# Scalar loads on another queue, the identity at the start, ten warming products and an early branch hint in a fused attention and two-layer gated kernel

## The chip, the cores and the metric

The kernel runs on one core of a Trainium2 chip. The metric is the device time of one execution in microseconds; three executions of the kernel before took 602.41, 602.73 and 602.85, the median is 602.73. One further execution was recorded by the hardware profiler: it took 602.38 us, of which the span of its instructions is 600.6 us; the remaining 1.78 us lie around the span.

## The reference

Three steps follow each other. Step one is masked softmax attention for 2 batches and 8 heads over 768 positions with 64 features per head. A query sees the first `n_sink` keys (4) and a causal window of `window` keys (128); both are scalar inputs, so the kernel has to load them before it can build a mask.

```python
scores = scale * np.matmul(q, k.transpose(0, 1, 3, 2))
keep = is_sink | in_window            # pos < n_sink, or 0 <= row - col < window
scores = np.where(keep, scores, -1e9)
a = np.exp(scores - max); a = a / (sum(a) + 1e-9)
x = np.matmul(a, v)                   # reshaped to 1536 tokens x 512
h = x @ w_in;  x = (h * tanh(softplus(h))) @ w_out      # 512 -> 2048 -> 512
h = x @ w2_in; out = (h * clip(h + 3, 0, 6) / 6) @ w2_out
```

## The kernel before

The 1536 rows are cut into twelve units of 128 query rows. Eight units (lists `first`) run in fp32 through `first_blocks()`; the other four run as a side task (`gen_units`) beside the first layer. For a unit of the first kind, `prep` transposes k and q on TensorE (PE) against an identity matrix `ident` (line 323), ScalarE (ACT) copies the transposes out of PSUM (line 326), `scores` multiplies them (line 350), VectorE (DVE) adds a mask and takes the maximum in one instruction (line 354), and ACT takes the exponential (line 358). `turn` and `values` transpose the probabilities and multiply by v (lines 369 and 393). The first unit in the list is unit 6, which starts its batch and so needs mask `m0` only.

The two layers that follow are split-precision fp16 products (lines 737 to 739 and 782 for the first layer, 806 to 808 and 846 for the second). Their weights arrive as fp64 words by DMA from SyncE's (SP's) queue and are decoded on DVE. This body is fully unrolled.

The head of the program, in the order of the code: a table load on ACT, three small constants by memset on DVE, then `emit_params` (lines 107 to 120), which issues two small broadcast loads of the scalars on SP and turns them into fp32 values `nsw` by seven small DVE instructions; then the loads of k, q and v of the first units and of the first weights, all on SP; then `warm`, a zeroed tile, and `NWARM` products of it (line 931) whose result nobody reads; then `emit_masks` (lines 122 to 153), which makes two index matrices on GpSimd (POOL), the identity and the masks on DVE. Four further products of `warm` stand behind the first unit's transposes (line 428).

The language has a scheduler. It keeps the instructions of an engine roughly in the order of the code, but lets one that is ready in its own simulated time go ahead of one that is not; the order on each engine is fixed when the program is built, and each engine then runs its instructions in that order. `tc.keep_in_program_order(x)` ties `x` behind what the code has already given to that engine. It ties nothing else.

The end of the program (lines 987 to 1012) reduces a number of checks into one integer `bad_i`. All five engines load it (`values_load`, line 1011) and branch on it (`tc.If(bad != 0)`, line 1012): where it is not zero, `general_path` recomputes everything in a slow general form; where it is zero, as with these inputs, every engine jumps past that code to a closing sequence of semaphore steps (reported at line 1216), in which SP waits for every other engine.

## Time and profile before

| what | value |
|---|---|
| median of three executions | 602.73 us |
| profiled execution | 602.38 us |
| its span | 600.6 us |
| PE busy | 579.9 us (97%) |
| DVE busy | 457.9 us (76%) |
| ACT busy | 398.3 us (66%) |
| POOL busy | 24.3 us (4%) |
| share of the chain that ended last, by engine | PE 65%, DVE 12%, issue 10%, ACT 8%, DMA 2%, POOL 2% |

Busy time counts the instructions that compute; branches, semaphore steps and the issue of DMAs are not counted, so an engine that is held in one of these shows as idle. A name like PEq, SPq or PEldq is the sequencer of that engine, which runs those uncounted instructions. The chain that ended last is followed back from the last computing instruction, so it doesn't reach into the closing sequence. A row of the timeline that ends in a bracket tells how long the engine was idle before it and what released it.

### The profile page before, as it was taken

The numbers are of one execution on the slowest core, as the hardware profiler recorded it, in microseconds if no ns is written. First come the engines' busy times: TensorE is split into PE (matmuls) and PEld (weight loads), VectorE is DVE, ScalarE is ACT, GpSimd is POOL, SyncE is SP. The second block draws the span as 40 slices with busy tenths as digits, with TensorE's granted clock in tenths as the row PEclk, the third lists the DMA queues.
The fourth block names the chain that finished last, engine by engine and source line by source line (L and its number), as shares of the span: only waits on it lengthen the run. The fifth ranks groups of instructions, "written<-read, shape, count | busy, mean of one in ns | idle before, by whom it ended". The sixth has DMA issues, their size and how long they took to land.

```text
span 600.6 us, 11389 instructions
## 1 busy us (share of the span) xinstructions
PE 579.9 (97%) x4430; PEld 395.0 (66%) x4430; DVE 457.9 (76%) x1102; ACT 398.3 (66%) x786; POOL 24.3 (4%) x36
## 2 busy tenths in 40 slices
PE   8999999999989999899989999999999999999995
PEld 5778764444445545444434468888888888888884
DVE  5689998999375454589999999866687889865753
ACT  5998887777687776679888886434354656543442
POOL 0041000700000000000000000000000000000000
PEclk9999999999999999999999999999999999999998
DMA  9876357997334433254544442000017676300001
GB/s 182 222 162 211 108 174 198 234 263 209 90 73 82 81 61 70 39 158 140 183 168 139 142 141 71 1 1 2 1 36 257 213 267 214 135 7 1 36 1 40
DMA packets 105843, 72.26 MB, mean 120 GB/s; under 512 B 73512, under 2 KB 98088, under 8 KB 105784
## 3 DMA queue, kind: packets, MB, share of 16 engines
q1 hardware_dynamic: 105784, 71.48, 42.4%
q8 instruction: 36, 0.59, 0.4%
q14 instruction: 23, 0.19, 0.1%
HBM read 60.43 MB, written 3.15 MB: 106 GB/s over the span
## 4 chain that ended last, share of the span: by engine, by line
PE 65%; DVE 12%; issue 10%; ACT 8%; DMA 2%; POOL 2%; SPq 0%; DVEq 0%; ACTq 0%
PE acc L846 18%; PE acc L782 9%; PE h L807 7%; PE h L806 7%; PE h L808 7%; PE h L737 3%; PE h L739 3%; PE h L738 3%; DVE g L754 2%; ACT d L358 1%; DVE p L212 1%; PE o L393 1%; DVE e L749 1%; DVE d L354 1%; ACT e L745 1%
## 5 line engine op out<-in xcount | busy, mean ns | idle before, releaser
L782 PE MATMUL acc<-g,w 128*128 128x512 f16 x576 | 131.2, 379 | 6.1 <-DVE g L754 5.4
L846 PE MATMUL acc<-w,g 128*128 128x256 f16 x1008 | 113.8, 273 | 0.0
L846 PEld LDWEIGHTS <-g 128*128 128x128 f16 x1008 | 98.6, 98 | 11.4
L806 PE MATMUL h<-xt,w 128*128 128x256 f16 x384 | 104.7, 273 | 0.0
L808 PE MATMUL h<-xt,w 128*128 128x256 f16 x384 | 104.7, 273 | 0.0
L807 PE MATMUL h<-xt,w 128*128 128x256 f16 x384 | 104.7, 273 | 0.0
L782 PEld LDWEIGHTS <-w 128*128 128x128 f16 x576 | 55.4, 98 | 72.2 <-issue 7.6
L737 PE MATMUL h<-xt,w 128*128 128x512 f16 x192 | 72.8, 379 | 1.9 <-DVE mins L558 1.2
L739 PE MATMUL h<-xt,w 128*128 128x512 f16 x192 | 72.8, 379 | 0.0
L738 PE MATMUL h<-xt,w 128*128 128x512 f16 x192 | 72.8, 379 | 0.0
L810 ACT ACTIVATE e<-h,bias 128x512 f32<-128x512 f32 x48 | 32.5, 678 | 54.5 <-PE h L808 54.5
L811 DVE SCALAR_TENSOR_TENSOR e<-e,h 128x512 f32<-128x512 f32 x48 | 32.8, 683 | 41.9 <-ACT e L810 41.9
L823 ACT ACTIVATE g<-e 128x256 f16<-128x256 f32 x96 | 29.5, 354 | 28.7 <-DVE e L811 28.7
L823 ACT ACTIVATE g<-sm 128x512 f16<-128x512 f32 x48 | 30.2, 629 | 27.5 <-DVE sm L818 27.4
L749 DVE SCALAR_TENSOR_TENSOR e<-e,h 128x512 f32<-128x512 f32 x48 | 30.7, 681 | 16.8 <-ACT e L747 16.7
L824 DVE SCALAR_TENSOR_TENSOR g<-sm,g 128x512 f16<-128x512 f32 x48 | 33.0, 688 | 11.0 <-ACT g L823 10.9
L807 PEld LDWEIGHTS <-w 128*128 128x128 f16 x384 | 37.6, 98 | 4.6
L806 PEld LDWEIGHTS <-w 128*128 128x128 f16 x384 | 37.6, 98 | 4.6
L808 PEld LDWEIGHTS <-w 128*128 128x128 f16 x384 | 37.6, 98 | 4.3
L212 DVE SCALAR_TENSOR_TENSOR p<-raw,y 128x1024 int32<-128x1024 int32 x32 | 39.4, 1232 | 0.4
L740 ACT ACTIVATE e<-h 128x512 f32<-128x512 f32 x48 | 28.1, 587 | 16.2 <-PE h L739 16.2
L754 DVE SCALAR_TENSOR_TENSOR g<-e,g 128x1024 f16<-128x1024 f32 x24 | 29.4, 1223 | 8.3 <-ACT g L753 8.3
(172 smaller groups left out, 935.6 us busy)
## 6 DMA issues: line engine op xcount, KB each, us to landing
raw<-in_moe_w_in_dram SPq DMA_DIRECT2D x48, 512.0 KB, 4.2
raw<-in_moe_w_out_dram SPq DMA_DIRECT2D x48, 512.0 KB, 4.9
out_dram<-ob SPq DMA_DIRECT2D x12, 256.0 KB, 2.6
first<-in_k_dram SPq DMA_DIRECT2D x8, 256.0 KB, 4.6
first<-in_q_dram SPq DMA_DIRECT2D x8, 256.0 KB, 4.5
first<-in_v_dram SPq DMA_DIRECT2D x8, 256.0 KB, 3.0
nk<-in_k_dram SPq DMA_DIRECT2D x5, 256.0 KB, 5.0
nv<-in_v_dram SPq DMA_DIRECT2D x5, 256.0 KB
```

Source lines behind the costliest of these rows:

```text
L212: nc.vector.scalar_tensor_tensor(out=p, in0=t[:, :, 1], scalar=3, in1=y, op0=ALU.logical_shift_left, op1=ALU.bitwise_xor)
L737: nc.tensor.matmul(o, wh, x[:, 0, c, :], start=c == 0, stop=False)
L738: nc.tensor.matmul(o, wh, x[:, 1, c, :], start=False, stop=False)
L739: nc.tensor.matmul(o, wl, x[:, 0, c, :], start=False, stop=c == KD - 1)
L749: nc.vector.scalar_tensor_tensor(out=e[:, i], in0=e[:, i], scalar=2.5, in1=hps[i], op0=ALU.subtract, op1=ALU.mult)
L754: nc.vector.scalar_tensor_tensor(out=gl, in0=e, scalar=sc, in1=gh, op0=ALU.mult, op1=ALU.subtract)
L782: nc.tensor.matmul(o, l_, r_, start=first and m == 0 and x == 0, stop=last and end and x == 2, skip_group_check=True)
L806: nc.tensor.matmul(o, wh, x[:, 0, c, :], start=c == 0, stop=False)
L807: nc.tensor.matmul(o, wh, x[:, 1, c, :], start=False, stop=False)
L808: nc.tensor.matmul(o, wl, x[:, 0, c, :], start=False, stop=c == KD - 1)
L823: nc.scalar.activation(out=g[:, 0, d_], in_=src, func=AF.Copy, scale=sc)
L846: nc.tensor.matmul(a[n // 2][:, n % 2], l_, r_, start=f == fa and m == 0 and n % 2 == 0 and x == 0, stop=ends and m == 1 and x == 2 and (n ...
```

## The change

It does four things. The two scalar loads are issued on ACT's queue instead of SP's, and `emit_params` stands ahead of ACT's table load and of the constants. The two index matrices and the identity are made by a new function `emit_ident`, which is the first thing in the code, with the matrix that the identity needs made first and the identity itself under `keep_in_program_order`; `emit_masks` gets the tile with the index matrices handed over. `NWARM` is 10 instead of 12. Last, a branch hint "likely taken" is placed on all five engines ahead of the warming tile, and tied by the label `end` to the branch at line 1012.

```diff
     def emit_params():
-            nc.sync.dma_start(out=raw[:, i, :], in_=a.bitcast(I32)...)
+            nc.scalar.dma_start(out=raw[:, i, :], in_=a.bitcast(I32)...)
...
-    def emit_masks():
+    def emit_ident():
+        tmp = part_p.tile([128, 4, 128], F32, tag="part", name="tmp")
+        col, rel = tmp[:, 0], tmp[:, 1]
+        nc.gpsimd.iota(rel, pattern=[[-1, 128]], base=0, channel_multiplier=1, ...)
+        tc.keep_in_program_order(nc.vector.tensor_scalar(out=ident, in0=rel, scalar1=0.0, scalar2=None, op0=ALU.is_equal))
+        nc.gpsimd.iota(col, pattern=[[1, 128]], base=0, channel_multiplier=0, ...)
+        return tmp
+
+    def emit_masks(tmp):
         ns, wd = nsw[:, 0:1], nsw[:, 1:2]
-        tmp = part_p.tile([128, 4, 128], F32, tag="part", name="tmp")
         col, rel, ind, dg = (tmp[:, i] for i in range(4))
-        nc.gpsimd.iota(col, ...)
-        nc.gpsimd.iota(rel, ...)
-        nc.vector.tensor_scalar(out=ident, in0=rel, scalar1=0.0, scalar2=None, op0=ALU.is_equal)
...
+    tmp_m = emit_ident()
+    emit_params()
     nc.scalar.preload_act_table_set("natural_log_exp_and_others")
     nc.vector.memset(one, 1.0)
     nc.vector.memset(fifth, 0.2)
     nc.vector.memset(bias3, 3.0)
-    emit_params()
     load_first(first[0], "kq")
...
+    tc.mark_branch_hint_location("end", hint="LikelyTaken", engines=[PE, DVE, Activation, Pool, SP])
     warm = part_p.tile([128, 512], F32, tag="part", name="warm").bitcast(F16)[:, 0:512]
...
-    emit_masks()
+    emit_masks(tmp_m)
...
-    with tc.If(bad != 0):
+    with tc.If(bad != 0, label="end"):
         general_path(tc, q, k, v, nsw, w1_in, w1_out, w2_in, w2_out, out)
...
-NWARM = 12
+NWARM = 10
```

## Rows read from the trace of the kernel before

**Rows 1.** The page, part 1: busy time, share of the span and instructions of each engine.
```profile
PE 579.9 (97%) x4430; PEld 395.0 (66%) x4430; DVE 457.9 (76%) x1102; ACT 398.3 (66%) x786; POOL 24.3 (4%) x36
```
**Rows 2.** Instructions around the end, line 1012: durations in ns (min/median/max), starts in us.
```profile
L1012 ACTq COMPARE_BRANCH  x1: 50/50/50, 596.1 to 596.1; - x1
L1012 PEldq COMPARE_BRANCH  x1: 3414/3414/3414, 596.1 to 596.1; - x1
...
L1012 PEldq EVENT_SEMAPHORE  x1: 51/51/51, 599.6 to 599.6; - x1
```
**Rows 3.** The same view of the closing sequence, line 1216.
```profile
L1216 SPq EVENT_SEMAPHORE  x10: 17/28/2127, 597.2 to 600.6; - x10
```
**Rows 4.** SP's own waits from 592 us on: total us, times, longest us.
```profile
SPq L1216 <- PEq L1012: 2.1, 1, 2.1
```
**Rows 5.** The page, part 3: packets, MB and share of the instruction queue q8.
```profile
q8 instruction: 36, 0.59, 0.4%
```
**Rows 6.** Chain that ended last, 0 to 30 us: start us, us, what.
```profile
1.27 5.30 PE wp L931 x12
6.57 0.98 PE tp L323 x8
7.55 0.86 PE wp L428 x4
...
9.20 1.65 ACT d L358 x8
```
**Rows 7.** Timeline of SP's DMA issues: start us, us of issue.
```profile
0.74 0.39 SPq L110 DMA_DIRECT2D raw<-in_n_sink_dram  x1
1.20 0.41 SPq L110 DMA_DIRECT2D raw<-in_window_dram  x1
1.66 0.43 SPq L293 DMA_DIRECT2D first<-in_k_dram  x1
2.12 0.58 SPq L293 DMA_DIRECT2D first<-in_q_dram  x1
2.75 1.23 SPq L293 DMA_DIRECT2D first<-in_k_dram  x1
```
**Rows 8.** DMA issues from 2.5 to 3 us: KB, median us to landing.
```profile
first<-in_q_dram SPq DMA_DIRECT2D x1, 256.0 KB, 4.3
first<-in_k_dram SPq DMA_DIRECT2D x1, 256.0 KB, 4.9
```
**Rows 9.** Line 323, PE's semaphore waits ahead of the first two units' transposes.
```profile
L323 PEldq EVENT_SEMAPHORE  x2: 51/51/51, 5.3 to 8.9; - x2
```
**Rows 10.** Timeline of ACT, DVE and POOL, 0 to 12 us.
```profile
0.73 1.28 ACT L912 ACT_TABLE_LOAD   x1 [0.73 <-PEq L1201]
0.94 0.27 DVE L928 MEMSET warm<- 128x256 uint32 x1
1.10 0.24 POOL L127 IOTA tmp<- 128x128 f32 x1
...
4.17 0.17 DVE L113 CAST f<-raw 128x4 f32<-128x4 int32 x1 [2.94 <-DMA raw<-in_window_dram]
...
5.91 0.22 DVE L128 TENSOR_SCALAR ident<-tmp 128x128 f32<-128x128 f32 x1
...
7.15 0.60 ACT L326 ACTIVATE kt<-tp 128x512 f32<-128x512 f32 x1 [5.13 <-PE tp L323]
7.21 0.23 DVE L135 TENSOR_SCALAR m<-tmp 128x128 f32<-128x128 f32 x1
...
7.64 0.59 ACT L326 ACTIVATE qt<-tp 128x512 f32<-128x512 f32 x1
...
8.87 0.29 DVE L354 CUSTOM_DVE_ANT_0 d<-s,m 128x128 f32<-128x128 f32 x1 [0.23 <-PE s L350]
```
**Rows 11.** Stretches: us, busy of PE, PEld, DVE, ACT, POOL; granted clock, DMA share, GB/s.
```profile
595.50:600.60 5.10, 0.00 (x0) 0.00 (x0) 0.01 (x1) 0.00 (x0) 0.00 (x0) 0.66 0.07 20
0.00:12.00 12.00, 10.18 (x54) 5.59 (x56) 6.42 (x48) 5.17 (x14) 0.70 (x7) 1.00 0.95 165
```

## Prediction

> **What bounds the kernel now.** I began with the busy shares: PE computes for 579.9 of 600.6 us, 97% [rows 1]. The reader is to see that the body can't give much without less PE work, and that the change takes only two products away from PE. So I looked at what isn't the body: the first 12 us and the last 5. For the end I read the line of the final branch, the line of the closing sequence and SP's own waits [rows 2 to 4]. The stretch from 595.5 us to the end holds no computing work at all [rows 11], yet it is 5.1 us long. PE's branch at 596.1 takes 3414 ns where ACT's takes 50 [rows 2], PE's next step is at 599.6, and SP, which gathers the engines, has one semaphore step of 2127 ns [rows 3], which is its wait of 2.1 us for PE [rows 4]. For the head I read the chain that ended last, the issues on SP and the timeline [rows 6, 7, 10]: the chain starts with twelve warming products from 1.27 to 6.57, then runs through the first unit's transposes, its scores and ACT's exponentials. The DMA engines are at 0.95 over the first 12 us [rows 11], so the head has two chains side by side, PE's warming and the loads.

> **The end.** The hint adds one instruction per engine near the start, and there nothing waits for it but the warming tile's memset, so I put it at nothing on PE and at most at a branch's 0.05 us [rows 2] on DVE. What it may remove is the long branch on PE: all five engines branch at 596.1, and the others are through in about 0.05 us. If PE were as quick, its semaphore step would come at about 596.1 + (599.6 - 596.1 - 3.41) + 0.05, that is before 596.3 instead of at 599.6. That isn't the gain. SP takes its steps one after another and reaches the one that waits for PE 2.13 us before that wait ends [rows 3]; what is late next is SP itself. The gain is therefore the wait, 2.1 us [rows 4], and not the 3.36 us by which PE's branch shortens. From below it is 0, if the early hint has no effect.

> That the 3.4 us are a fetch of code is argued from three rows: the branch alone is long on PE, PE has by far the longest program (4430 products and as many weight loads [rows 1]), and the queue q8 carried 36 packets in 0.59 MB, 16 KB each [rows 5], which as a stream over the span is what a long program would ask for. [...]

> **The head.** *Scalar loads.* On SP the two scalar loads hold the queue from 0.74 to 1.66 [rows 7]. Without them the first k load is issued at 0.74, 0.92 us earlier, and every load behind it on SP moves with it. Today the first q, issued at 2.12, lands 4.3 us later at 6.4, the second unit's k, issued at 2.75, 4.9 us later at 7.65 [rows 7, 8], and PE waits for loads at 5.3 and again at 8.9 [rows 9]. All of that can move by up to 0.92. The DMA engines are full in this stretch [rows 11], so the flow moves as a whole. On ACT the two issues come ahead of the table load, 0.92 us; that load ends then at about 0.73 + 0.92 + 1.28 = 2.9, and ACT's first use is at 7.15 after 5.13 us idle [rows 10]: hidden. If it were not, it would cost the 0.92.

> *The scalars themselves* now share the DMA engines with the k load. Today the conversion on DVE starts at 4.17 and mask `m0` is finished at 7.21 + 0.23 = 7.44; it is used first at 8.87 [rows 10]. It has 1.4 us of slack. At best the scalars land as today; at worst behind the two loads that are now issued beside them, 2 x 1.23 us later (1.23 = 7.65 - 6.42, one load after another [rows 7, 8]), and `m0` comes at 9.9, a loss of 1.0 against today. Queued behind the waiting conversion on DVE are the masks and the first unit's `L354`, and ACT waits for these. The nearest row is the `window` load itself, 2.9 us from issue to use [rows 7, 10]; with half a load's delay `m0` is at 8.0, still ahead of an L354 that has moved forward by 0.5 to 8.4, and I take no loss.

> *Warming and the identity.* Twelve products take 5.30 us, 0.43 each; the four behind the transposes 0.86, 0.22 each [rows 6]. [...] The granted clock is printed as 1.00 for the whole head [rows 11], so here I go by the pace. Two products fewer are 2 x 0.43 = 0.86 us. Against it stands the identity: if DVE really does it ahead of the memset of `warm`, the memset waits for an index matrix on POOL (0.24) and for `ident` (0.22), so the warming starts up to 0.46 later [rows 10]; and if the scheduler lets the memsets go first, 0. The transposes, which follow the warming without a gap [rows 6], so start 0.40 to 0.86 earlier, at 5.5 to 6.0. Today `ident` is ready at 5.91 + 0.22 = 6.13 [rows 10], so without the edit it would be the next to hold them; made early, it is out of the way. The k load would be there at 5.3 - 0.92 = 4.4 and q at 5.5.

> [...]

> ACT copies the transposes at 7.15 and 7.64, and the scores, the maximum (8.87) and the exponentials (9.20) hang on the second copy [rows 6, 10]. Bounds of the head: +0.92 (everything moves with SP) and -1.0 (masks late). I take 0.5 us, from the middle of 0.2 to 0.86. I expect it to stay to the end, since loads, PE, ACT and DVE all move the same way and PE is full behind them.

> **Sum.** Against the profiled execution's 602.38 (span 600.6 and 1.78 around it): 602.38 - 2.1 - 0.5 = 599.8. That execution is 0.35 below the median of three, 602.73, so the time to compare is 599.8 + 0.35 = about 600.1.

> **Rivals.** (1) *The hint has no effect*: a block fetched on it is gone, or never fetched, when the branch comes. For it speak the 36 blocks that pass through the queue [rows 5]; against it that a hint which is tied to one branch by name should be kept until that branch is fetched. PE's branch stays at 3.4 us and the head alone is left: 602.73 - 0.5 = 602.2. (2) *The other side: the hint misleads the fetch.* If PE's sequencer goes for the hinted block at its first block end instead of for the next one, PE stalls there for as long as at its branch today, 3.41 us [rows 2], and since PE is full from then on [rows 1] the stall is not hidden; the hinted block is used up long before the end, so the branch stays long as well. 602.73 + 3.4 - 0.5 = 605.6. It decides if at one of the first ends of PE's blocks a gap of over 3 us stands on PE that isn't there now; nothing in this trace shows a hint, so I can't exclude it. (3) *The masks turn late* with the scalars behind the loads: 602.73 - 2.1 + 1.0 = 601.6 with a hint that works. What speaks against it is the slack of 1.4 us [rows 10].

> **How the numbers follow.** Forecast 0.60; no effect 0.22; misled fetch 0.11; late masks or an order of the scheduler's that costs about as much 0.07. Some 0.2% (1.2 us) is what a measurement of this kernel can tell from no change: faster means below 601.5, slower above 603.9. The forecast's own range is 599.3 to 601.1: a head that gives 0.92 instead of 0.5 makes 599.7, and the three executions shown lie 0.44 apart; a head that loses half of its lower bound, 0.5, makes 601.1. All of it is faster. No effect is the same, late masks are between, misled is slower: faster 0.62, same 0.26, slower 0.12. The range for all reaches from 599.3 over the second case to 602.6, and leaves out the misled fetch and the edges.

> **What would show it.** Right: PE's branch at line 1012 falls from 3414 to under 200 ns; SP's wait for PE in the closing sequence is gone, and the stretch after `bad_i` is about 3.0 us instead of 5.1; the first k load is issued at about 0.74; the transposes of line 323 start at 5.5 to 6.0 and ACT's first exponential at about 8.7. Wrong: a branch of 3.4 us again (first rival); a gap of microseconds on PE, 10 to 30 us from the start, that is not there now (second); a mask instruction on DVE as the releaser of `L354` (third). If the branch is short and the time has fallen by over 3 us, I have mistaken SP's steps for a bound that they aren't.

## The result and the profile after

The changed kernel takes 607.86 us (median of four, 605.67 to 608.95) against 602.57 for the kernel before: 1.0088 times as long, 95% interval 1.0067 to 1.011. It is slower, and its four executions spread over 3.3 us, those of the kernel before over 0.8 (over 1.4 to 2.5 us in the 9 to 23 executions taken beside the later runs). The profiled execution is the fastest of the four, 605.67 us with a span of 603.9. What is read from it below therefore accounts for 605.67 - 602.38 = 3.3 us of a loss of 5.3; the other three have a mean granted clock of 0.995 against its 0.998, and no profile shows where they lost the rest. The forecast of 600.1 missed; so did the range. The other-side rival's number, 605.6, is near the profiled execution's by chance: its mechanism is not what happened.

**The end did what was forecast.** Line 1017 is the branch now and line 1221 the closing sequence; the columns are those of [rows 2, 3].
```profile
L1017 ACTq COMPARE_BRANCH  x1: 68/68/68, 601.4 to 601.4; - x1
...
L1017 PEldq COMPARE_BRANCH  x1: 385/385/385, 601.5 to 601.5; - x1
...
L1221 SPq EVENT_SEMAPHORE  x10: 17/28/28, 602.6 to 603.8; - x10
...
L1221 PEldq BRANCH_PREFETCH_HINT  x1: 50/50/50, 0.8 to 0.8; - x1
```
PE's branch is down from 3414 ns to 385, and SP's longest step from 2127 ns to 28: the wait for PE [rows 4] is gone. The hint that did it was issued 600 us earlier, in 50 ns. The instruction queue q8 carried 35 packets instead of 36 [rows 5]: behind the last computation there is one where there were two. The stretch behind the last computation, as in [rows 11]:
```profile
600.80:604.00 3.20, 0.00 (x0) 0.00 (x0) 0.04 (x1) 0.00 (x0) 0.00 (x0) 0.53 0.09 30
```
It is 3.1 us long (up to 603.9) where it was 5.1.

**The head went the other way.** The timeline of the changed kernel, in order of time, for [rows 6, 7, 10]:
```profile
0.83 0.46 SPq L296 DMA_DIRECT2D first<-in_k_dram  x1
...
1.25 0.45 ACTq L110 DMA_DIRECT2D raw<-in_window_dram  x1
...
1.35 4.45 PE L936 MATMUL wp<-warm 128*128 128x512 f16 x10 [1.35 <-DVE ones L1002]
...
5.36 0.17 DVE L113 CAST f<-raw 128x4 f32<-128x4 int32 x1 [4.06 <-DMA raw<-in_window_dram]
...
6.83 0.22 DVE L126 TENSOR_SCALAR ident<-tmp 128x128 f32<-128x128 f32 x1
...
7.10 1.97 PE L326 MATMUL tp<-ident,first 128*128 128x128 f32 x8 [1.30 <-DVE ident L126]
...
8.86 1.84 PE L431 MATMUL wp<-warm 128*128 128x512 f16 x4
...
10.64 0.71 PE L353 MATMUL s<-kt,qt 64*128 64x128 f32 x8
```
The first k load did leave SP 0.83 us earlier. But the scalars landed 1.2 us later (conversion at 5.36, before at 4.17), and `ident` still stands behind the scalars' conversion on DVE, at 6.83. The reader is to see the bracket at 7.10: PE had finished its ten products and stood idle for 1.30 us for `ident`. Then it ran slowly: the transposes took 1.97 us and the four products 1.84. The same view of the kernel before:
```profile
6.37 1.19 PE L323 MATMUL tp<-ident,first 128*128 128x128 f32 x8
7.39 1.03 PE L428 MATMUL wp<-warm 128*128 128x512 f16 x4
```
In the changed kernel these four products start some 0.43 us apart, the lower pace, that of the twelve in [rows 6]; the four there take 0.22 each, the upper pace. What the expectations say of PE's clock in the head is read from these two paces: the granted clock is printed as 1.00 for the first 12 us here too, and no trace shows that a clock is behind them. The first scores start at 10.64 instead of 8.34.

**More was lost where nothing was edited.** Stretches of both kernels, columns as in [rows 11]; first the kernel before:
```profile
12.00:75.00 63.00, 59.84 (x590) 47.44 (x591) 52.93 (x187) 56.62 (x170) 10.84 (x17) 1.00 0.68 179
...
120.00:160.00 40.00, 38.94 (x200) 17.60 (x199) 30.13 (x43) 29.64 (x42) 0.00 (x0) 1.00 0.81 211
```
and the changed kernel:
```profile
12.00:75.00 63.00, 58.17 (x585) 47.08 (x584) 51.82 (x189) 55.77 (x169) 9.67 (x16) 1.00 0.65 171
...
120.00:160.00 40.00, 36.75 (x188) 16.30 (x187) 34.81 (x49) 28.22 (x40) 0.00 (x0) 1.00 0.91 237
```
PE is 1.7 us less busy in the fp32 attention stage and 2.2 us less from 120 to 160 us. By the start of the first product of the first layer (72.5 us before, 76.4 now) the lag has grown from 2.3 to 3.9 us, by 175 us to 5.7; at the end of the computing it is 5.3, and the end gives 2.0 back: 3.3. The traces show why to look there: up to 150 us the order of the instructions differs on all five engines, although the code there is the same. Of the kernels below, e1 (the hint alone) and e3 (all edits but the queue) have the order of before behind the head, and e2 (the queue alone) has that of the changed kernel. So it is the move of the two loads to ACT's queue that makes the scheduler choose another order.

### The profile page after: what moved, and what is told of

Its sections match the earlier page's. It is cut to its first block, busy times and chain, and to the rows that moved or that the text cites. A ratio compares the mean times of both kernels' runs of the same rounds, so it can differ in the third digit from the quotient of the medians.

```text
span 603.9 us, 11390 instructions
## 1 busy us (share of the span) xinstructions
PE 581.6 (96%) x4428; PEld 396.1 (66%) x4428; DVE 457.3 (76%) x1102; ACT 398.4 (66%) x786; POOL 18.8 (3%) x36
## 4 chain that ended last, share of the span: by engine, by line
PE 61%; DVE 12%; issue 11%; ACT 10%; DMA 3%; POOL 1%; SPq 1%; ACTq 0%; DVEq 0%; POOLq 0%
PE acc L849 18%; PE h L811 7%; PE h L809 7%; PE h L810 7%; PE acc L785 6%; PE h L740 3%; PE h L742 2%; PE h L741 2%; ACT e L748 2%; DVE p L215 2%; ACT e L749 2%; PE o L396 2%; PE s L353 2%; DVE g L757 2%; PE tp L372 1%
```

## The experiments

Theory A: the hint gains 2 us; the head loses through late scalars, an identity that waits for them and PE's idle time; the rest is lost by the new order of the body. The rivals B, C, D and A2 stand in the expectations. Times are medians of five or more executions, ratios against the kernel before on the same chip (602.0 to 602.4).

**Parts of the change alone.** e1 adds the hint and the label to the kernel before; e2 only moves the queue; e3 is the changed kernel with the queue moved back; e4 has four more products.
```diff
e1, to the kernel before
+    tc.mark_branch_hint_location("end", hint="LikelyTaken", engines=[...])
-    with tc.If(bad != 0):
+    with tc.If(bad != 0, label="end"):
e2, to the kernel before
-            nc.sync.dma_start(out=raw[:, i, :], ...)
+            nc.scalar.dma_start(out=raw[:, i, :], ...)
e3, to the changed kernel
-            nc.scalar.dma_start(out=raw[:, i, :], ...)
+            nc.sync.dma_start(out=raw[:, i, :], ...)
e4, to the changed kernel
-NWARM = 10
+NWARM = 14
```
e1. 

> The kernel before with the branch hint alone; the order of every engine's other instructions is that of before. Theory A (the hint works, the loss sits in the head and in the body's new order): PE's branch at the end under 0.5 us instead of 3.41, SP's wait for PE gone, time 602.6 - 2.1 = 600.5. Rival (the hint costs something in the body, by fetching at the wrong place): above 601.5, with gaps on PE at block ends that the kernel before doesn't have.

599.74 us, 0.9956 (0.9942 to 0.997): 2.4 us faster. PE's branch:
```profile
L1013 PEldq COMPARE_BRANCH  x1: 394/394/394, 596.1 to 596.1; - x1
```
The hint alone gives the whole gain of the end, and nothing is lost in the body: the computing ends by 595.5 us, as before.

e2. 

> The kernel before with the two scalar loads on ACT's queue and nothing else: twelve products, no hint. The scheduler gives this kernel the changed kernel's order in the body. Theory A: the scalars land 1.2 us late (5.4), the identity behind them at 7.1, PE idle about 0.7 us behind twelve products, and the new order of the attention stage costs 3 us more: 606 to 608. Rival B (the loss is all of the warming: ten products and the late clock; the order costs nothing): only the 0.7 us gap is left, 603.0 to 604.

608.94 us, 1.011 (1.0093 to 1.0127): the queue's move alone takes longer than the whole change, which has the hint in it. Rival B, the warming, is out as the whole cause: here there are twelve products. In the profiled execution PE waits for `ident` too, but its pace had risen before that, during the warming. Its twelve products took 4.34 us, where ten took 4.45 in the changed kernel and twelve 5.30 in [rows 6]:
```profile
1.27 4.34 PE L931 MATMUL wp<-warm 128*128 128x512 f16 x12 [1.27 <-DVE ones L997]
...
7.28 1.09 PE L323 MATMUL tp<-ident,first 128*128 128x128 f32 x8 [1.67 <-DVE ident L128]
8.21 1.03 PE L428 MATMUL wp<-warm 128*128 128x512 f16 x4
```
It lost more later: between 145 and 152 us PE waited 1.1 and 2.0 us for `g`, and then the granted clock is lower, 0.83 in the mean from 150 to 160 us:
```profile
150.00:160.00 10.00, 8.23 (x32) 3.44 (x32) 6.10 (x8) 5.75 (x7) 0.00 (x0) 0.83 0.55 108
```

e3. 

> The changed kernel with the scalar loads back on SP's queue: ten products, identity and masks moved, hint kept. The scheduler gives it the order of before in the body. Theory A: scalars at 4.2, identity at 5.9, PE idle about 0.3 us behind ten products, the hint's 2.1 us saved: 600.0 to 601.0. Rival B (ten products are too few and the clock rises late): 602 to 604 with the first transposes and the four products behind them at the slow pace.

599.36 us, 0.9957 (0.9942 to 0.9972), a little below the expected span. Three of the four edits together are a gain, but no more than the hint's alone (e1): neither a gain of the other two nor a cost of ten products behind scalars that land in time can be seen.

e4. 

> The changed kernel with fourteen warming products instead of ten, which fill PE's idle 1.30 us ahead of the first transposes; all else and every other engine's order as in the changed kernel. Theory A: the clock rises during the warming, the transposes take about 1.2 us instead of 2.0 and the four products 1.0 instead of 1.8, but the order stays: 604 to 605.5, and the spread of the changed kernel's runs (605.7 to 609.0) shrinks below 1 us. Rival B (all of the loss is the warming): 601.0 to 602.

605.63 us, 1.006 (1.0044 to 1.0076), 2.2 below the changed kernel. PE has no idle time now, and its pace is the upper one, 1.03 us for the four products:
```profile
7.30 1.04 PE L326 MATMUL tp<-ident,first 128*128 128x128 f32 x8
8.17 1.03 PE L431 MATMUL wp<-warm 128*128 128x512 f16 x4
9.13 0.71 PE L353 MATMUL s<-kt,qt 64*128 64x128 f32 x8
```
The first scores come 1.5 us sooner than in the changed kernel. So the idle time with the lower pace behind it is about 2 us of the loss, and 3.5 us above the kernel before remain, more with the hint's gain added. The spread did not shrink below 1 us as expected (604.13 to 606.99). In this profile the hint gave only part of its gain:
```profile
L1017 PEldq COMPARE_BRANCH  x1: 1723/1723/1723, 598.7 to 598.7; - x1
```
SP's wait in line 1017 was 1.8 us instead of 0.5, and q8 carried 36 packets again, one of them at 597.5, just ahead of the branch. In the profiles of all other kernels with the hint PE's branch took 380 to 394 ns and q8 carried 35. Why e4 differs, and whether its other executions do, is open; the 2.2 us may be short by up to 1.3.

**Order and queue apart.** In e5 and e6 every instruction of the first stages gets an edge behind the one that shall precede it on its engine, by instruction numbers taken from the other program (a list `ORDER`; the programs have the same instructions). All calls then pass through line 41, which is what their profiles show.
```diff
+    nc = _Nc(tc)
...
+            if ins is not None and ins.name in BEHIND:
+                info = mybir.DependencyInfo(mybir.DependencyClass.NoSync, mybir.DependencyReason.DATA)
+                self._tc.add_manual_dep(ins, BEHIND[ins.name], info, reason="order")
...
+BEHIND = {f"I-{b}": f"I-{a}" for v in ORDER.values() for a, b in zip(v, v[1:])}
```
e5. 

> The kernel of e3 (scalars on SP, 599.4) with edges that force on every engine the order which the changed kernel's instructions have; nothing else differs. Theory A (the order that the scheduler chose when the scalars left SP costs time by itself): the head as in e3, then 1 us lost by 90 us and another by 160 us, as e4 lost them: 601.0 to 602.5. Rival C (the order is harmless; what follows the head in the changed kernel is the late scalars or the loads on two queues): 598.8 to 600.0.

e6. 

> The changed kernel (scalars on ACT, ten products, 607.9) with edges that force on every engine the order of e3, which in the body is that of before. Theory A: scalars at 5.4, identity at 6.8, PE idle 1.3 us and the clock late, so the head is 0.7 to 2.3 late, but nothing is lost behind it: 600.5 to 603. Rival C: 605 to 608, since the order doesn't matter.

| hint, ten products | old order | new order |
|---|---|---|
| scalars on SP | e3 599.36 | e5 604.95 (ratio 1.0036 to 1.0066) |
| scalars on ACT | e6 601.53 (0.9976 to 1.000) | changed kernel 607.86 |

The order costs 5.6 us with the one queue and 6.3 with the other, more than theory A expected; the queue 2.2 and 2.9. The four kernels ran on different chips: by the ratios, each to the kernel before on its own chip, the order costs 5.7 and 6.0 and the queue 1.9 and 2.2. Rival C is refuted in both rows. The edges by themselves cost nothing: e8 below has them on e3's own order and is no slower than e3. e5 is the clean case: its first scores start at 8.06, those of e3 at 8.07. It is 1.9 us behind e3 at the first product of the first layer and 4.4 from 150 us on. e3 in stretches, then e5:
```profile
12.00:75.00 63.00, 59.82 (x589) 47.27 (x587) 53.44 (x187) 56.51 (x168) 11.10 (x17) 1.00 0.69 181
...
120.00:160.00 40.00, 39.39 (x202) 17.84 (x201) 29.96 (x43) 30.27 (x42) 0.00 (x0) 1.00 0.78 206
```
```profile
12.00:75.00 63.00, 58.30 (x580) 46.99 (x577) 52.53 (x183) 55.31 (x165) 9.67 (x16) 1.00 0.70 184
...
120.00:160.00 40.00, 36.53 (x187) 16.20 (x186) 32.78 (x47) 28.58 (x40) 0.00 (x0) 1.00 0.85 218
```
The same two stretches lose as in the changed kernel. PE's waits from 120 to 160 us in e3, and then in e5 (total, times, longest):
```profile
PE acc L785 <- DVE g L757: 0.6, 1, 0.6
```
```profile
PE acc L41 <- DVE g L41: 2.5, 2, 2.0
PE h L41 <- DVE mins L41: 0.6, 1, 0.6
PE acc L41 <- ACT g L41: 0.4, 1, 0.4
```
The second half of a product's input (`g`) comes late from DVE. Ahead of it DVE decodes weights, and there it stands still for a load:
```profile
144.53 0.77 DVE L41 TENSOR_SCALAR y<-raw 128x1024 int16<-128x1024 int16 x1 [1.17 <-DMA raw<-in_moe_w_out_dram]
```
That this is the cause of the longer wait is argued from DVE's order, and not tested.

**The identity and the masks.** e7 and e8 force one thing more: `ident` ahead of the conversion on DVE. In e9 the first unit's first four maxima also go ahead of some of the masks for other units and of the checks.
```diff
DVE's order in e7 and e8, by line
-113 115 116 117 118 119 120 992 993 994 126 133
+126 113 115 116 117 118 119 120 992 993 994 133
DVE's order in e9
+126 133 113 115 116 117 118 119 120 134 137 138 135 143 144 357 357 357 357 140 141 145 146 152 154 153 155 156 992 993 994
```
e7. 

> As e6, and the identity forced ahead of the scalars' conversion on DVE, which is what the change meant. Theory A (the head is lost because the identity stays behind the late scalars): first transposes at 5.6 directly behind the warming, no idle PE, 598.5 to 599.5, and a spread below 1.5 us. Rival D (the scalars' own lateness binds, by the masks): no better than e6, 600.5 to 603, with DVE's masks as releaser of line 357.

e8. 

> The kernel of e3 with the identity forced ahead of the scalars' conversion on DVE; order otherwise that of e3. Theory A: the identity is ready at 1.5; the transposes then start when ten products end, 5.6, or when k lands, 5.4, instead of 6.0: 598.8 to 599.4. Against e7 it shows what moving the loads forward by 0.9 us is worth once the identity is out of the way: theory A says e7 ahead by 0 to 0.5.

e9. 

> As e7 (scalars on ACT, identity first, old order, 600.2), and on DVE the first unit's first four maxima forced ahead of the masks that other units use and of the checks of the scalars. Theory A (with the scalars on ACT the maxima are held by DVE's queue of mask instructions in front of them, not by m0 itself): the first maximum at about 8.2 instead of 9.35, held by PE's scores; 598.6 to 599.6. Rival (the loads on two queues or something later holds e7): 599.9 to 600.4, as e7.

e7: 600.16 us, 0.9974 (0.9965 to 0.9983), 1.4 below e6, though short of theory A's span. The transposes start at 5.17 with no wait for `ident`; both theories had a part. e6, then e7:
```profile
7.05 1.97 PE L41 MATMUL tp<-ident,first 128*128 128x128 f32 x8 [1.25 <-DVE ident L41]
```
```profile
5.17 0.60 PE L41 MATMUL tp<-ident,first 128*128 128x128 f32 x4
...
6.31 0.66 PE L41 MATMUL tp<-ident,first 128*128 128x128 f32 x4 [0.54 <-DMA first<-in_q_dram]
...
7.76 0.71 PE L41 MATMUL s<-kt,qt 64*128 64x128 f32 x8
8.01 0.23 DVE L41 TENSOR_SCALAR m<-tmp 128x128 f32<-128x128 f32 x1
...
9.21 0.23 DVE L41 TENSOR_SCALAR m_all<-tmp 128x128 f32<-128x128 f32 x1
9.35 0.28 DVE L41 CUSTOM_DVE_ANT_0 d<-s,m 128x128 f32<-128x128 f32 x1
```
The scores were ready at about 8.2 and `m0` at 8.24, but the first maximum came at 9.35: it stood in DVE's queue behind masks that it doesn't use. That is rival D in a sharper form. The q load, issued at 1.36, released PE only at 6.31; in e8, where it is issued at 2.23, it does so at 6.66. Of 0.87 us on the queue 0.35 are left.

e8: 599.18 us, 0.9957 (0.9945 to 0.997), as expected, and no faster than e3 beyond the spread. Theory A's order of the two was wrong: e7 is not ahead of e8 but 1.0 behind.

e9: 598.98 us, 0.9952 (0.9939 to 0.9966), 1.2 below e7 as expected, and the fastest median of all:
```profile
7.33 0.23 DVE L41 TENSOR_SCALAR m<-tmp 128x128 f32<-128x128 f32 x1
...
7.74 0.71 PE L41 MATMUL s<-kt,qt 64*128 64x128 f32 x8
...
8.26 0.29 DVE L41 CUSTOM_DVE_ANT_0 d<-s,m 128x128 f32<-128x128 f32 x1
```

**Which engine's order?** Two mixtures, made as e5 is, with the new order on some engines only.
```diff
e10: ORDER of SP from the changed kernel, the rest from e3
e11: ORDER of PE, DVE, Activation and Pool from the changed kernel, SP from e3
```
e10. 

> The kernel of e3 (599.4) with the changed kernel's order forced on SP's queue alone, that is for the loads; the computing engines keep the order of e3. Theory A1 (the loss of e5, 605.0, comes from the computing engines' order): 599.0 to 600.5. Rival A2 (it comes from weight loads that stand behind others): 602.5 to 605.

e11. 

> The kernel of e3 with the changed kernel's order forced on PE, DVE, ACT and POOL, while SP's loads keep the order of e3. Theory A1: 602.5 to 605, as e5. Rival A2: 599.0 to 601.

e10 took 613.91 us (1.0176 to 1.0204) and e11 607.01 (1.0054 to 1.0082); neither theory allowed for both being worse than e5. In the attention stage the answer is clear: from 12 to 75 us e10 keeps e3's pace, e11 loses as e5 did. e10, then e11:
```profile
12.00:75.00 63.00, 59.84 (x590) 47.21 (x587) 53.42 (x187) 56.40 (x169) 11.16 (x17) 1.00 0.69 181
75.00:120.00 45.00, 39.11 (x220) 19.84 (x219) 36.73 (x54) 31.03 (x41) 9.28 (x10) 0.94 0.53 154
```
```profile
12.00:75.00 63.00, 58.61 (x581) 47.12 (x579) 52.84 (x183) 55.60 (x166) 9.67 (x16) 1.00 0.70 186
75.00:120.00 45.00, 40.70 (x228) 20.59 (x227) 38.59 (x60) 32.34 (x45) 6.25 (x5) 0.97 0.63 174
```
So that part, 1.7 to 1.9 us by the start of the first layer, belongs to the computing engines' order. From 75 us on the mixtures lose 15 and 6 us, where e5 loses 2.5. With loads and decoding in unlike orders ACT, which decodes and converts, stands still for a load; e10, then e11:
```profile
102.69 0.63 ACT L41 ACTIVATE k<-nk 128x512 f16<-128x512 f32 x1 [8.80 <-DMA nk<-in_k_dram]
```
```profile
111.91 0.63 ACT L41 ACTIVATE q<-nq 128x512 f16<-128x512 f32 x1 [5.60 <-DMA nq<-in_q_dram]
```
PE then waits 4.5 and 2.7 us for ACT's `g`, and the clock that is granted from 75 to 120 us is 0.94 and 0.97, which may be a part of these losses. Which engine's order costs e5 its 2.5 us stays open.

## Why the prediction was wrong

*The end: right.* The step was 2.1 us, SP's wait and not the branch's length; e1 measured 2.4. Only the sign "under 200 ns" was not met: the branch took 385. The first rival is refuted by these 385 ns, and the misled fetch by e1, which loses nothing in the body; e4's 1723 ns, with one packet more on q8, show that part of the gain can still be lost. That the long branch is a fetch of code stays the prediction's argument; the changed kernel's profile adds to it one packet behind the last computation instead of two.

*"Every load behind it on SP moves with it", "the flow moves as a whole" and "I expect it to stay to the end": the step that failed most.* I treated the body's program as fixed. It isn't: two loads leaving SP gave the first 150 us another order, on every engine (e2). e3 against e5 and e6 against the changed kernel put 5.6 and 6.3 us on it, where my sum had a gain of 0.5 us kept to the end. I gave an order of the scheduler's a share of 0.07, at about 1 us. Some of the 5.6 to 6.3 us may be clock: the executions of e4, e5 and the changed kernel have a mean granted clock of 0.993 to 0.998, those of e1, e3, e8 and e9 of 0.997 to 1.000, and in e4 and e5 the slower ones mostly have the lower clock. How much, no profile of a slower execution shows.

*"Made early, it is out of the way": failed.* I weighed whether the identity or the memsets go first, and not that the identity might not move. `keep_in_program_order` ties it behind what stands before it, and nothing stood there; nothing ties the conversion behind it. It kept its place behind the scalars, and PE waited for it: the transposes started at 7.10 and not at 5.5 to 6.0, ACT's first exponential at 11.49 and not at 8.7. e6 to e7, where it does move, is 1.4 us.

*The scalars: mis-sized.* I bounded their delay at 0 to 2.5 us and took 0.6; it was 1.2. The delay then met the two things above.

*The masks' slack of 1.4 us: wrong.* I compared `m0`'s end with the first maximum. In the kernel before DVE ran six mask instructions between the two, from 7.35 to 8.64; the bracket of the maximum's row in [rows 10], idle 0.23, was the slack. e7 against e9 shows the price: 1.1 us at the first maximum, 1.2 in the time.

*The loads' 0.92 us: mostly not there.* Between e8 and e7 q is issued 0.87 us sooner and releases PE 0.35 sooner. Nor did PE wait for loads at 5.3 and 8.9 before: [rows 9] has two steps of 51 ns, and PE's waits in the first 12 us name no load.

*Ten products.* Two fewer cost nothing that can be seen while the transposes follow (e3). With PE idle for 1.30 us in front of them, as in the changed kernel, the pace stayed the lower one as well; e4 puts the idle time and the pace together at 2.2 us. I took the head's 0.5 us from the middle of 0.2 to 0.86. No run shows the term of 0.2; what the runs show in its place is a pace that didn't rise at one point: ten products took 4.45 us in the profile of the changed kernel, all at the lower pace, and 3.98 in that of e7.

## What to carry to other kernels

Where a scheduler orders the instructions, a moved DMA is a change to the whole program: compare each engine's order before and after, before any sum is made, and hold the order fixed to learn what the edit itself costs. A pin on one instruction says nothing about those that follow it in the code; to put X ahead of Y, tie Y. The slack of a result is read from the consumer's own idle time, not from the moment at which the result was finished: in e7 `m0` was finished at 8.24, and DVE came to the maximum at 9.35, behind masks that it doesn't use. Of this change the hint is shown to be worth keeping (e1, 599.74 us). With the scalars on SP the other two edits do no harm (e3, 599.36), and e9, with the masks in the order of their use, has the lowest median (598.98), but the intervals of e1, e3, e8 and e9 overlap.
